# A fused attention and two-layer expert kernel: the expert layer's work list is written anew, and one unit's output is computed in another form

## The chip, the cores and the metric

The kernel runs on one core of one Trainium2 chip. Its metric is the device time of one execution in microseconds: 1166.03 us, the median of three runs (1165.91 to 1166.03).

## The reference, cut to what matters

Three layers follow each other. The first is attention over pooled memories (batch 4, 8 heads, 576 positions), and its result is `x` with 2304 tokens of 512 features. The second is a wide layer with a cosine gate. The third, the expert layer, is the one that the change is about:

```python
def _moe2_ref(x, domain_probs, w1, w2):      # x [2304, 512], w1 [4, 512, 1024], w2 [4, 1024, 512]
    p = domain_probs / (domain_probs.sum(-1, keepdims=True) + 1e-09)
    out = np.zeros((N, D), dtype=np.float32)
    for e in range(E):
        h = np.maximum(x @ w1[e], 0.0)
        out += p[:, e:e + 1] * (h @ w2[e])
    return out
```

## The kernel before, in words

Each product of two fp32 matrices is made of three TensorE passes over a high and a low part of each factor (`mm3`, line 500): high by high, high by low, low by high. A low part is a subtraction on VectorE (DVE) or GpSimd (POOL), a high part a copy on ScalarE (ACT).

The expert layer cuts the hidden features of all experts into 16 slices `s` of 256 features, the tokens into two halves `u` of 1152, and each half into two blocks `j` (512 and 640 tokens). That makes 64 units, worked through one after the other. A unit has four kinds of task, and their names are the words of a list:

- `H12` (`hidden`) makes the hidden activations of unit 12 with seven TensorE products of six matmuls each (256 or 320 columns). `R12` (`rectify`) applies the relu.
- `P12` (`pair_prep`) makes from these, on ACT, DVE and POOL, the seven operands `ht` that the output needs, each split into a high and a low part. `Q12.2` does the same for a single token tile.
- `O12.0` and `O12.1` (`pair_out`) each make the output of two token tiles of 128 tokens with seven products of three matmuls of 256 columns, in place of two full ones: sums of some operands are multiplied instead. Their order in TensorE's queue is m1, m5, m6, m2, m7, m3, m4. They accumulate in one PSUM tile `op` with the quarters pz, px and py. Three DVE instructions (`gather`, line 1274) read that tile, scale by the token's expert share and add to the sum `acc` in SBUF: e1 stands between m2 and m7 and reads px and py, e2 between m3 and m4 reads the same two, e3 after m4 reads pz and px. So m7, which adds to px again, has to wait for e1, and m4 for e2. In a profile m5, m6, m7 and m3 read `op<-wt,ht`, and m1, m2 and m4 read `op<-wb,ht`.
- `O12.2` (`plain_out`) makes the output of one token tile in full, with six matmuls of 512 columns and one `gather`. A unit that `WHOLE` names (line 306) has all of its four or five tiles worked in this way, without a `P` task: units 0, 30 and 31 of the 64.

Other words are the splitting of the input for a half (`X01`, `X10`, `X11`), of weights in the first half (`wa11`, `wb11`, `Ea8`, `Eb8`), and weights' transfers on SP's DMA queue (`get..`, `keep..`, `fetch..`). In the first half the split weights are also stored in DRAM, and the second half only loads them.

What sets the order is `LIST` (line 134), written out by hand or by a search: some 3600 words, each of which issues the next instruction or instruction group of its task. A stroke behind a word (`P3'`) takes DVE in place of POOL for a step that may go to either. So `LIST` fixes every engine's queue; each engine works its queue in order, and the waits between engines are set when the program is built, from the tiles that the instructions read and write. The tasks also name what they depend on (the last arguments of `gather`, `either`, `pe`); in the listed stage these names serve whoever makes the list, and `have(...)` only says before which point a word may not stand.

Of the kernel before, what the change touches and what calls it, by code (L numbers as in the profile page):

```python
# [138 lines left out]
P2 P2' H3 H3 H3 P2 Q2.2 Eb7 O1.1 H3 O1.1 Eb7 O1.0 Eb7' O1.0 H3 O1.0 Eb7 Ea7 Eb8 H3 R3 O1.1 Ea7 keepwb0 O1.0 O1.1 O1.1
Q2.2 O1.0 R3 R3 O1.1 Ea7 O1.0 R3 O1.1 H3 P2 O1.1 O1.0 R3 O1.1 Ea7 O1.0 H4 O1.1 Ea7 O2.0 O2.0 Ea7' O2.1 O2.0 O2.1 P3'  # L140
Ea7 Ea7 O2.0 P3 keepwt0 O2.0 P3' O2.1 O2.2 Ea7' P3 P3 O2.0 Ea7 O2.1 O2.2 H4 H4 P3 P3 P3 Ea7 P3 H4 H4 O2.1 O2.1 O2.1 P3
O2.1 Ea7 O2.0 O2.1 O2.0 H4 H4 Q3.2 O2.0 P3 Ea7 Ea7 O2.1 O2.0 H4 getwb2 O2.0 Ea7 getwa3 H4 O2.1 getwt2 O3.0 H4 R4 Ea7
# [297 lines left out]
def tile_kernel(  # L440
# [854 lines left out]
    def make_wa(s):  # L1295
# [10 lines left out]
        for f in mixes:  # L1306
            o4 = yield either(416, 740, f, o, t1, free=BW[s > TURNS[0] // 2])
# [76 lines left out]
    def early(s, kind, before):  # L1384
# [491 lines left out]
```

## Time and profile before

| what | value |
|---|---|
| median of three runs | 1166.03 us |
| the profiled execution | 1163.89 us |
| its span, first to last instruction | 1162.1 us |
| TensorE matmuls (PE) busy | 1119.0 us, 96% |
| VectorE (DVE) busy | 870.7 us, 75% |
| ScalarE (ACT) busy | 624.8 us, 54% |
| GpSimd (POOL) busy | 582.5 us, 50% |
| the expert layer, in the span | from 378.3 to the end |
| its first half of tokens | 378.3 to 764.6 |

PE stands for TensorE's matmuls and PEld for its weight loads, which run ahead of them. A matmul's busy time includes its way through the array, so matmuls that follow each other overlap and PE looks busy across short pauses; the idle time before a weight load shows a pause more fully. A row of the timeline merges instructions of one kind that follow each other; the bracket is the idle time of that engine before it and who ended it.

### The profile page before, as it was taken

The numbers are of one execution on the slowest core, as the hardware profiler recorded it, in microseconds if no ns is written. First come the engines' busy times: TensorE is split into PE (matmuls) and PEld (weight loads), VectorE is DVE, ScalarE is ACT, GpSimd is POOL, SyncE is SP. The second block draws the span as 40 slices with busy tenths as digits, with TensorE's granted clock in tenths as the row PEclk, the third lists the DMA queues.
The fourth block names the chain that finished last, engine by engine and source line by source line (L and its number), as shares of the span: only waits on it lengthen the run. The fifth ranks groups of instructions, "written<-read, shape, count | busy, mean of one in ns | idle before, by whom it ended". The sixth has DMA issues, their size and how long they took to land.

```text
span 1162.1 us, 22606 instructions
## 1 busy us (share of the span) xinstructions
PE 1119.0 (96%) x8971; PEld 1067.8 (92%) x8971; DVE 870.7 (75%) x1344; ACT 624.8 (54%) x1297; POOL 582.5 (50%) x577
## 2 busy tenths in 40 slices
PE   9999999999999999999999999999999999999996
PEld 8689999999999999998989899999999999999995
DVE  5888989897888765788777877776757766566664
ACT  4886665566555654555646655454454544444451
POOL 1465555665677357556656684335252333323350
PEclk9999999999999999999999999999999999999999
DMA  9932556267300889698785486374533643336422
GB/s 313 369 91 57 173 173 217 68 210 263 142 19 1 308 337 375 246 350 288 259 310 191 174 308 231 120 289 158 218 136 140 233 172 136 137 145 237 172 73 82
DMA packets 58553, 230.08 MB, mean 198 GB/s; under 512 B 6992, under 2 KB 17744, under 8 KB 44112
## 3 DMA queue, kind: packets, MB, share of 16 engines
q1 hardware_dynamic: 58448, 228.65, 54.5%
q8 instruction: 70, 1.15, 0.4%
q14 instruction: 35, 0.29, 0.1%
HBM read 158.63 MB, written 69.99 MB: 197 GB/s over the span
## 4 chain that ended last, share of the span: by engine, by line
PE 89%; DVE 6%; DMA 2%; issue 1%; POOL 0%; SPq 0%; ACT 0%; DVEq 0%; POOLq 0%; ACTq 0%
PE op L503 49%; PE hp L503 33%; DVE acc L1274 4%; PE z L503 4%; PE vw_ps L790 1%; DVE ht L551 1%; DMA q<-in_qt_dram 1%; DMA kv<-in_kv_dram 1%; PE warm L926 1%; DMA raw<-in_w_out_dram 1%; PE kvp L674 0%; DVE acc L551 0%; PE sc L727 0%; SPq L531 0%; DVE wt L551 0%
## 5 line engine op out<-in xcount | busy, mean ns | idle before, releaser
L1274 DVE SCALAR_TENSOR_TENSOR acc<-op,p_all,acc 128x512 f32<-128x512 f32 x390 | 283.9, 746 | 151.3 <-PE op L503 149.0
L503 PE MATMUL hp<-x,wa 128*128 128x256 f32 (+1 forms) x2268 | 354.3, 296 | 0.9 <-DVE c L1260 0.9
L503 PEld LDWEIGHTS hp<-x,wa 128*128 128x128 f32 x2268 | 316.1, 188 | 2.7 <-DVE c L1260 1.1
L503 PE MATMUL op<-wt,ht 128*128 128x256 f32 x1440 | 228.8, 285 | 24.1 <-DVE acc L1274 21.5
L503 PEld LDWEIGHTS op<-wt,ht 128*128 128x128 f32 x1440 | 195.9, 188 | 37.0 <-DVE acc L1274 33.8
L503 PE MATMUL op<-gt,wo 128*128 128x288 f32 x1536 | 218.1, 296 | 0.0
L503 PEld LDWEIGHTS op<-gt,wo 128*128 128x128 f32 x1536 | 208.1, 188 | 4.7 <-issue 2.4
L503 PE MATMUL op<-wb,ht 128*128 128x256 f32 (+1 forms) x1194 | 205.2, 294 | 5.4 <-DVE acc L1274 4.9
L503 PEld LDWEIGHTS op<-wb,ht 128*128 128x128 f32 x1194 | 171.8, 188 | 12.1 <-DVE acc L1274 6.5
L534 ACT ACTIVATE c<-c 128x256 f32<-128x256 f32 (+1 forms) x122 | 53.7, 444 | 186.8 <-DVE c L1260 186.6
L551 POOL TENSOR_TENSOR sm<-c,sm 128x256 f32<-128x256 f32 x65 | 54.5, 838 | 130.2 <-DVE sm L551 103.6
L503 PE MATMUL hp<-attnT,vw 128*128 128x288 f32 x768 | 113.2, 296 | 0.3 <-DVE attnT L551 0.3
L503 PEld LDWEIGHTS hp<-attnT,vw 128*128 128x128 f32 x768 | 105.2, 188 | 3.5 <-issue 1.6
L551 POOL TENSOR_TENSOR ht<-sm,ht 128x512 fp32r<-128x512 f32 x66 | 91.7, 1393 | 32.8 <-ACT ht L534 32.7
L551 POOL TENSOR_TENSOR gt<-y,gt 128x576 fp32r<-128x576 f32 x41 | 60.1, 1466 | 78.2 <-ACT gt L534 75.3
L897 DVE TENSOR_TENSOR acc<-op,acc 128x576 f32<-128x576 f32 (+1 forms) x120 | 84.9, 711 | 17.3 <-PE op L503 15.9
L551 POOL TENSOR_TENSOR ht<-c,ht 128x256 fp32r<-128x256 f32 (+1 forms) x68 | 70.7, 1045 | 41.5 <-ACT ht L534 41.5
L534 ACT ACTIVATE ht<-sm 128x512 fp32r<-128x512 f32 x120 | 73.9, 625 | 13.0 <-POOL sm L551 8.5
L551 POOL TENSOR_TENSOR sm<-c 128x512 f32<-128x512 f32 x21 | 27.3, 1302 | 90.8 <-ACT c L534 72.2
L534 ACT ACTIVATE u<-hp 128x320 f32<-128x320 f32 (+1 forms) x126 | 50.2, 407 | 38.7 <-PE hp L503 38.1
L1260 DVE TENSOR_TENSOR c<-hp,u 128x320 f32<-128x320 f32 (+1 forms) x126 | 56.3, 452 | 18.2 <-PE hp L503 17.0
L534 ACT ACTIVATE ht<-c 128x512 fp32r<-128x512 f32 (+2 forms) x128 | 63.0, 517 | 6.0 <-PE op L503 4.9
(152 smaller groups left out, 1558.7 us busy)
## 6 DMA issues: line engine op xcount, KB each, us to landing
wa<-wa_d SPq DMA_DIRECT2D x27, 1792.0 KB, 8.5
wb<-wb_d SPq DMA_DIRECT2D x27, 1024.0 KB, 7.3
wt<-wt_d SPq DMA_DIRECT2D x27, 1024.0 KB, 7.2
wa_d<-wa SPq DMA_DIRECT2D x10, 1792.0 KB, 11.4
raw<-in_w_dram SPq DMA_DIRECT2D x32, 512.0 KB, 6.7
wt_d<-wt SPq DMA_DIRECT2D x10, 1024.0 KB, 10.5
wb_d<-wb SPq DMA_DIRECT2D x10, 1024.0 KB, 8.4
wa_d<-acc SPq DMA_DIRECT2D x18, 512.0 KB, 4.4
```

The lines of the kernel that those rows point to most:

```text
L503: nc.tensor.matmul(out=ps, lhsT=lt(a), rhs=rt(b), start=first and i == 0, stop=last and i == 2, skip_group_check=more,)
L534: return Op("ACT", ns, fn or (lambda: nc.scalar.activation(out=out, in_=in_, func=func, **kw)), *deps, table=table)
L551: eng.tensor_tensor(out=out, in0=in0, in1=in1, op=op)
L790: nc.tensor.matmul(out=ps[32 * i:32 * i + 32, g, j * FS:j * FS + FS], lhsT=kvT[b][64 * g:64 * g + 64, 1, i, :], rhs=wi[s][0][64 * g:64 * g ...
L897: e = yield dve(155 + 301 * nd, lambda: nc.vector.tensor_tensor(out=dst, in0=op[:, :, :TH], in1=dst, op=ALU.add), o)
L926: nc.tensor.matmul(out=warm[:, :128], lhsT=ones, rhs=ones, start=True, stop=True)
L1260: return dve(157 + 1.045 * n, lambda: nc.vector.tensor_tensor(out=out, in0=ps, in1=sb, op=ALU.add), *deps)
L1274: nc.vector.scalar_tensor_tensor(out=dst, in0=ps, scalar=pe, in1=dst, op0=ALU.mult, op1=ALU.add)
```

## The change

Three things change, and nothing before the expert layer's list.

`LIST` is another list of the same tasks. One unit fewer is named in `WHOLE`: unit 30, the last slice but one, 640 tokens, first half, now has two pairs and one single tile in place of five full ones. And the tasks name more dependences: e1 of a pair names m2 beside m6, a gather into a token tile names the gather of the slice before it, and has to stand behind it, the four sums of a weight name each other, and the two tiles that unit 1 borrows name a few more of their readers.

```diff
 LIST = """
-X01 H0 X01 H0 park H0 Eb7 H1 H0 X01' H0 H0 X01' H0 H0 H0 X01 H0 X01' X01 H1 X01 H0 R0 R0 H0 R0 H1 H1 H1 keepwa0 R0
...
-WHOLE = ((0, 0, 0), (0, 14, 1), (0, 15, 1))
+WHOLE = ((0, 0, 0), (0, 15, 1))
...
+        o4 = None
         for f in mixes:
-            o4 = yield either(416, 740, f, o, t1, free=BW[s > TURNS[0] // 2])
+            o4 = yield either(416, 740, f, o, t1, o4, free=BW[s > TURNS[0] // 2])
...
-                R["raw2"].give(kr, Join([o4, lo]))
-        R["te"].give(kt, lo)
+                R["raw2"].give(kr, Join([o4, *los]))
+        R["te"].give(kt, Join(los))
...
-        c22 = yield sum_(n, c[:, 1, n:], px[:, :n], u3, o7, a5, tc_)
+        c22 = yield sum_(n, c[:, 1, n:], px[:, :n], u3, o7, a5, tc_, *([o3] if i == 1 else []))
...
-        g = yield gather(DM, outv[:, ti, :], op, p_, s == 0, o, done["x", u, 1])
+        if s:
+            yield have(("sum", ti, s - 1))
+        g = yield gather(DM, outv[:, ti, :], op, p_, s == 0, o, done["x", u, 1], done.get(("sum", ti, s - 1)))
+        todo.set(("sum", ti, s), g)
...
         m2 = yield prod(pz, 1, 1)
-        e1 = yield gather(DM, db, duo[:, 2 * HD2:], pb, first, m6)
+        if s:
+            yield have(("sum", ib, s - 1))
+        e1 = yield gather(DM, db, duo[:, 2 * HD2:], pb, first, m6, m2, done.get(("sum", ib, s - 1)))
         m7 = yield prod(px, 4, 5, e1)
...
-        e3 = yield gather(DM, da, duo[:, HD2:3 * HD2], pa, first, m4)
+        if s:
+            yield have(("sum", ia, s - 1))
+        e3 = yield gather(DM, da, duo[:, HD2:3 * HD2], pa, first, m4, done.get(("sum", ia, s - 1)))
+        todo.set(("sum", ia, s), e3)
```

What the new list does is read from the order of the built programs. The first place is TensorE's queue at unit 5's first pair. Before, its tile is `op_5853` and that of the unit's second pair `op_5888`; `hp` and `z` are products of `H6`:

```order
L503 MATMUL op_5853<-wt_5552,ht_5720 128x256 x3
L503 MATMUL op_5888<-wt_5552,ht_5720 128x256 x3
L503 MATMUL hp_5841<-x_5014,wa_5543 128x320 x6
L503 MATMUL op_5853<-wb_5539,ht_5720 128x256 x3
L503 MATMUL op_5853<-wt_5552,ht_5720 128x256 x6
L503 MATMUL op_5888<-wt_5552,ht_5720 128x256 x3
```

The first row is m6, the fourth m2, and the fifth m7 with m3: m7 stood directly behind m2.

In the new list the same pair has the tile `op_5886`, the second pair `op_5918`, and `op_5961` is the unit's single tile:

```order
L504 MATMUL op_5886<-wt_5562,ht_5733 128x256 x3
L504 MATMUL op_5918<-wb_5566,ht_5733 128x256 x3
L504 MATMUL hp_5823<-x_5013,wa_5497 128x320 x6
L504 MATMUL op_5918<-wt_5562,ht_5733 128x256 x3
L504 MATMUL hp_5815<-x_5014,wa_5497 128x320 x6
L504 MATMUL op_5918<-wt_5562,ht_5733 128x256 x3
L504 MATMUL op_5918<-wb_5566,ht_5733 128x256 x3
L504 MATMUL op_5886<-wb_5566,ht_5733 128x256 x3
L504 MATMUL op_5961<-wb_5566,h1_5774 128x512 x6
L504 MATMUL op_5886<-wt_5562,ht_5733 128x256 x6
```

Now a whole single tile of six 512-column matmuls stands between m2 (the eighth row) and m7 (the last).

The second place is TensorE's queue at unit 48, in the second half. Before, `op_11671` is the first pair and `op_11685` the second:

```order
L503 MATMUL op_11685<-wt_11415,ht_11572 128x256 x3
L503 MATMUL hp_11717<-x_9166,wa_11428 128x256 x6
L503 MATMUL op_11685<-wb_11452,ht_11572 128x256 x3
L503 MATMUL op_11671<-wb_11452,ht_11572 128x256 x3
L503 MATMUL op_11685<-wt_11415,ht_11572 128x256 x6
```

The second pair's m2 is the third row and its m7 the fifth: one product, the first pair's m4, stood between them.

In the new list the pairs are `op_11692` and `op_11771`:

```order
L504 MATMUL op_11771<-wt_11470,ht_11604 128x256 x3
L504 MATMUL op_11771<-wb_11493,ht_11604 128x256 x3
L504 MATMUL op_11692<-wt_11470,ht_11604 128x256 x3
L504 MATMUL hp_11745<-x_9284,wa_11482 128x256 x6
L504 MATMUL op_11692<-wt_11470,ht_11604 128x256 x3
L504 MATMUL op_11771<-wt_11470,ht_11604 128x256 x6
```

Two pair products and one product of `H50` now stand between the second pair's m2 (second row) and its m7 (last row).

The third place is the end of DVE's queue. Before, `op_13483` and `op_13509` are the pairs of unit 62, the other tiles single ones of unit 63, and the last TensorE product of the program is the m4 that writes `op_13509`:

```order
L1274 SCALAR_TENSOR_TENSOR acc_70<-op_13509,p_all_78,acc_70 128x2x256
L1274 SCALAR_TENSOR_TENSOR acc_70<-op_13570,p_all_78,acc_70 128x512
L1274 SCALAR_TENSOR_TENSOR acc_70<-op_13483,p_all_78,acc_70 128x512
L1274 SCALAR_TENSOR_TENSOR acc_70<-op_13581,p_all_78,acc_70 128x512
L1274 SCALAR_TENSOR_TENSOR acc_70<-op_13509,p_all_78,acc_70 128x512
```

Only the last of these five reads what the last product wrote.

In the new list the pairs of unit 62 are `op_13501` and `op_13538`, and the last TensorE product is the m4 that writes `op_13501`:

```order
L1275 SCALAR_TENSOR_TENSOR acc_70<-op_13583,p_all_78,acc_70 128x512
L1275 SCALAR_TENSOR_TENSOR acc_70<-op_13501,p_all_78,acc_70 128x512
L1275 SCALAR_TENSOR_TENSOR acc_70<-op_13616,p_all_78,acc_70 128x512
L1275 SCALAR_TENSOR_TENSOR acc_70<-op_13538,p_all_78,acc_70 128x512
L1275 SCALAR_TENSOR_TENSOR acc_70<-op_13604,p_all_78,acc_70 128x512
L1275 SCALAR_TENSOR_TENSOR acc_70<-op_13594,p_all_78,acc_70 128x512
```

Now the gather that needs the last product is the fifth from the end, and four stand behind it.

## Rows read from the trace of the kernel before

**Rows 1.** The page: the span; each engine's busy time, share, instructions.
```profile
span 1162.1 us, 22606 instructions
PE 1119.0 (96%) x8971; PEld 1067.8 (92%) x8971; DVE 870.7 (75%) x1344; ACT 624.8 (54%) x1297; POOL 582.5 (50%) x577
```

**Rows 2.** By stage: PE, PEld, DVE, ACT, POOL busy; granted clock, DMA share, GB/s.
```profile
0.00:378.30 378.30, 374.67 (x3472) 350.91 (x3473) 319.40 (x510) 237.77 (x375) 220.80 (x235) 1.00 0.48 161
378.30:764.60 386.30, 366.87 (x2705) 352.90 (x2704) 293.98 (x447) 209.36 (x488) 219.36 (x209) 1.00 0.74 268
764.60:1153.90 389.30, 377.49 (x2797) 364.00 (x2795) 255.59 (x386) 177.67 (x434) 142.30 (x135) 1.00 0.43 163
```

**Rows 3.** The page's weight-load groups: busy, mean ns | idle before, releaser.
```profile
L503 PEld LDWEIGHTS op<-wt,ht 128*128 128x128 f32 x1440 | 195.9, 188 | 37.0 <-DVE acc L1274 33.8
...
L503 PEld LDWEIGHTS op<-wb,ht 128*128 128x128 f32 x1194 | 171.8, 188 | 12.1 <-DVE acc L1274 6.5
```

**Rows 4.** Who waited for whom: us in total, times, longest.
```profile
PEld op L503 <- DVE acc L1274: 40.3, 58, 2.0
```

**Rows 5.** Timeline, unit 5's first pair: start, us, engine [idle before].
```profile
457.17 0.87 PE L503 MATMUL op<-wt,ht 128*128 128x256 f32 x6
...
458.76 0.52 PE L503 MATMUL op<-wb,ht 128*128 128x256 f32 x3
459.31 0.75 DVE L1274 SCALAR_TENSOR_TENSOR acc<-op,p_all,acc 128x512 f32<-128x512 f32 x1 [2.24 <-PE op L503]
...
460.12 1.13 PEld L503 LDWEIGHTS op<-wt,ht 128*128 128x128 f32 x9 [1.05 <-DVE acc L1274]
...
461.30 0.52 PE L503 MATMUL op<-wb,ht 128*128 128x256 f32 x3
```

**Rows 6.** Timeline, unit 48's two pairs and the products behind them.
```profile
976.53 0.77 PEld L503 LDWEIGHTS op<-wt,ht 128*128 128x128 f32 x6 [0.34 <-DVE acc L1274]
...
979.13 0.87 PE L503 MATMUL op<-wb,ht 128*128 128x256 f32 x6
...
980.49 0.78 PEld L503 LDWEIGHTS op<-wt,ht 128*128 128x128 f32 x6 [0.70 <-DVE acc L1274]
...
981.32 1.04 PE L503 MATMUL hp<-x,wa 128*128 128x320 f32 x6
...
982.20 0.87 PE L503 MATMUL op<-wb,ht 128*128 128x256 f32 x6
...
982.90 0.88 PE L503 MATMUL hp<-x,wa 128*128 128x256 f32 x6
```

**Rows 7.** Timeline: m7 of two pairs, three pair products between.
```profile
620.48 0.77 PEld L503 LDWEIGHTS op<-wt,ht 128*128 128x128 f32 x6 [0.39 <-DVE acc L1274]
...
693.91 1.12 PEld L503 LDWEIGHTS op<-wt,ht 128*128 128x128 f32 x9 [1.08 <-DVE acc L1274]
```

**Rows 8.** Timeline, unit 12's first pair: its m4, with DVE and POOL.
```profile
543.66 1.72 POOL L551 TENSOR_TENSOR ht<-sm,ht 128x512 fp32r<-128x512 f32 x1
...
544.17 1.49 DVE L551 TENSOR_TENSOR ht<-c,ht 128x256 fp32r<-128x256 f32 x1
...
546.37 0.42 PEld L503 LDWEIGHTS op<-wb,ht 128*128 128x128 f32 x3 [1.80 <-DVE acc L1274]
```

**Rows 9.** Timeline, unit 32: hidden products, first operand on POOL.
```profile
768.85 2.52 PE L503 MATMUL hp<-x,wa 128*128 128x256 f32 x18
...
773.82 1.75 POOL L551 TENSOR_TENSOR ht<-c,ht 128x512 fp32r<-128x512 f32 x1
```

**Rows 10.** Timeline, the end: the last PE and DVE rows.
```profile
1151.99 1.91 PE L503 MATMUL op<-wb,ht 128*128 128x512 f32 x9
1152.19 3.38 DVE L1274 SCALAR_TENSOR_TENSOR acc<-op,p_all,acc 128x512 f32<-128x512 f32 x5 [0.70 <-PE op L503]
```

**Rows 11.** Timeline: a DVE step on 128x256 in the turn of the halves.
```profile
772.55 0.43 DVE L551 TENSOR_TENSOR sm<-c,sm 128x256 f32<-128x256 f32 x1
```

**Rows 12.** The 50 us with most DMA in the expert layer; DMA stands last.
```profile
400.00:450.00 50.00, 47.64 (x356) 46.06 (x355) 33.67 (x56) 28.14 (x68) 29.82 (x30) 1.00 0.93 341
```

More of the change, by code (lines that the diff above doesn't have):

```diff
@@ L210 @@
-O28.1 X10 H30 O28.1 R30 X10 R30 O29.0 X10 X10 O29.0 R30 O29.1 O29.0 O29.1 R30 O29.0 O29.1 R30 O29.0 R30 X10' O29.1
-O29.1 O29.0 H31 H31 O29.1 H31 H31 R30 O29.1 X10' O29.1 H31 H31 X10 O29.1 X10 H31 O29.1 fetchwa0 O29.0 O29.0 O29.1
-O29.0 H31 H31 O29.0 O29.0 H31 R31 R31 O30.0 R31 R31 X11 R31 R31 X11' O30.1 R31 X11 O30.0 O30.2 O30.1 O30.3 X11' O30.2
-X11 O30.4 X11' X11 X11 O30.3 H32 O30.4 fetchwb0 fetchwa1 O31.0 fetchwt0 X11' fetchwt1 H32 H32 X11 H32 X11' X11 H32 H32
-X11 O31.0 H32 X11 H32 H32 X11 H32 R32 H32 R32 R32 R32 R32 P32' P32 O31.1 P32' P32 P32 P32 O31.2 O31.1 P32 P32 P32'
@@ new lines @@
+R1 O0.0 Eb7 O0.1 O0.3 P1' P1 Eb7 O0.2 Eb7 H2 P1' H2 Eb7 Eb7 O0.3 P1 P1 H2 Ea7 H2 H2 Eb7' P1 H2 P1' Eb7 H2 Eb7 H2 P1
+P1' P1' H2 P1 H2 R2 H2 R2 R2 Eb7' R2 O1.0 H3 getwa2 R2 P2' P2 Eb7 O1.0 Eb7 H3 P2 H3 Eb7' O1.1 P2 P2 O1.0 P2 H3 Eb7
+Ea7' H3 Eb8 O1.0 O1.1 Ea7 O1.0 O1.0 Ea7 O1.1 O1.0 H3 H3 O1.1 Q2.2 P2' P2 P2 O1.1 H3 Ea7 O1.1 O1.0 Q2.2 O1.0 H3 H3 R3
+Ea7 O1.1 Ea7 O1.0 O1.1 R3 R3 O1.1 P2 Ea7 O1.0 O1.1 P2 H4 Ea7 R3 O1.0 O1.1 H3 O1.1 Ea7' O2.0 R3 O2.1 Ea7 P3 P3 O2.0
+keepwb0 O2.1 O2.0 keepwt0 O2.2 O2.1 P3 O2.0 O2.1 P3 P3 Ea7 P3 P3' O2.2 H4 H4 Ea7' P3 O2.0 P3' Q3.2 Ea7 H4 H4 getwa3
@@ new lines @@
+O9.0 O9.1 Ea9' P10 P10 P10 O9.2 O9.0 Ea9 Ea9 getwa6 P10' H11 H11 Ea9 P10 P10' O9.0 O9.1 Ea9 H11 Eb10 O9.1 O9.2 H11
+O9.1 P10' O9.0 Eb10' H11 H11 O9.0 Eb10 P10' O9.1 Eb10 O9.0 O9.1 H11 O9.0 Eb10 O9.1 O9.1 Eb10 H11 O9.1 H11 R11 O10.0
+Eb10 Eb10 Eb10 O10.0 R11 R11 Ea10 O9.1 R11 H11 getwb6 O9.1 O10.0 Eb10 O10.0 R11 O10.0 P11 P11 O10.1 O10.0 H12 Eb10
+Q11.2 O10.1 P11 O10.0 Q11.2' H12 H12 O10.1 P11' P11 P11 H12 Eb10' H12 O10.1 P11' Eb10 Eb10 O10.1 Eb10 O10.0 O10.1 H12
+H12 P11 O10.0 H12 Eb10 Ea10' getwa7 O10.1 Ea10 O10.1 H12 H12 R12 P11 O10.0 H12 P11 P11' O10.1 R12 R12 O10.0 O10.1 R12
@@ new lines @@
+P19 Q19.2' H20 P19 O18.0 P19 P19 O18.1 O18.1 H20 H20 O18.1 P19 P19 O18.1 Ea15 O18.0 H20 O18.0 P19 O18.1 P19 O18.0
+O18.1 O18.0 H20 H20 R20 Ea15 O18.0 O18.1 O18.1 O18.0 O18.1 wa11 wb11 getwt10 H21 Ea15 R20 R20 wa11 O18.0 O18.1 H20
+O18.1 wa11 O19.0 O19.0 wa11' wa11 R20 R20 O19.1 P20' P20 O19.1 O19.2 P20' O19.1 wa11 O19.0 wa11 wa11' wa11 P20' O19.1
+O19.1 P20 H21 wa11 O19.1 H21 P20 O19.2 O19.0 O19.0 wa11 O19.1 O19.0 H21 H21 P20' P20 O19.0 P20' P20 O19.0 H21 H21 P20
+O19.0 O19.1 H21 O19.1 O19.0 O19.1 O19.0 H21 wb11 wa12 wb11 wb11 wb11' O20.0 H21 wb11 R21 O20.0 R21 H21 O20.0 O19.1
@@ new lines @@
+wb12 P22 wb12 wb12 O21.0 H23 wb12' wb12 wb12' wb12 H24 R23 O21.1 R23 O22.0 R23 O22.0 wb12' R23 O22.1 O22.1 P23' P23
+H24 O22.1 P23' O22.0 O22.1 Q23.2 wb12' H24 O22.1 O22.0 wa13 wb13 keepwb11 O22.0 H24 H24 wa13 H24 P23 P23 P23 P23'
+O22.0 O22.1 H24 O22.0 wa13' O22.0 P23 O22.1 P23' wa13 H24 wa13 O22.0 O22.1 P23 H24 O22.1 P23 O22.0 H24 R24 wa13 wa13
+O22.1 O22.0 H24 O22.1 O23.0 keepwt11 O23.0 Q23.2' keepwa12 O23.1 R24 R24 O23.0 O23.1 wa13' R24 O23.2 R24 P24' P24
+O23.1 wa13' P24 H25 P24 P24 P24 H25 H25 P24 P24 H25 H25 O23.0 P24 O23.1 O23.1 H25 H25 O23.1 P24 O23.2 O23.0 P24 O23.1
@@ new lines @@
+O27.0 O27.1 O27.0 O27.1 H29 O27.1 O27.0 O27.1 H29 H29 R29 O27.0 O27.1 getwt15 H29 getwb15 R29 R29 O28.0 R29 O28.1 R29
+O28.0 P29 P29 H30 O28.0 O28.1 O28.0 P29 O28.0 H30 P29 P29 H30 P29 P29' O28.1 O28.0 H30 P29 P29' H30 H30 H30 O28.0
+O28.1 O28.1 H30 O28.1 P29' O28.0 O28.1 O28.0 O28.1 H30 H30 R30 O28.1 H30 R30 R30 P29' R30 O28.0 R30 O28.1 O28.0 H31
+P30 P30 Q30.2 O29.0 Q30.2' O29.0 P30 H31 O28.1 P30' P30 O29.0 H31 P30 O29.0 P30' O29.1 P30 O29.1 P30' O29.0 H31 H31
+O29.1 O29.0 P30' P30 X10 O29.1 O29.0 X10' O29.1 O29.0 O29.1 X10 H31 H31 O29.0 O29.1 X10' O29.1 O29.0 O29.0 O29.1 X10
@@ new lines @@
+H31 O29.0 O29.1 X10 X10 H31 fetchwa0 H31 X10' O30.0 O29.1 O30.0 X10 O29.1 H31 O30.0 R31 O30.0 R31 fetchwa1 X10 O30.1
+R31 O30.1 X10' X10 O30.0 R31 O30.2 X10 O30.0 O30.1 X10 R31 R31 X10' O30.1 O30.0 R31 O30.1 O30.0 X10' O31.0 O30.1 X10
+O30.0 X10 O30.1 O30.2 O30.1 O30.0 O30.1 O31.1 X11 O30.0 X11 O31.0 O31.2 O31.1 X11' O30.1 O31.3 fetchwt0 O30.1 X11
+fetchwt1 O31.2 O31.0 O31.4 fetchwb0 O31.3 X11 O31.1 O31.2 H32 X11' X11 O31.3 H32 X11' H32 H32 H32 X11' H32 H32 O31.4
+X11 H32 O31.4 X11 X11 H32 fetchwb1 H32 R32 H32 R32 R32 X11' R32 H33 R32 P32' P32 H33 H33 P32' H33 P32' P32 P32 P32'
@@ new lines @@
+H33 H33 H33 P32 P32' H33 P32' X11 P32' H33 X11' X11' H33 R33 X11 R33 X11' O32.0 O32.0 O32.1 O32.1 H33 O32.0 R33 O32.0
+R33 R33 O32.0 H34 O32.0 P33' H34 H34 P33 P33 H34 O32.1 P33 P33 H34 H34 P33 P33 P33 O32.0 P33' O32.0 H34 O32.1 P33
+O32.1 H34 O32.1 H34 H34 R34 P33' O32.1 R34 R34 O32.1 H34 O32.0 R34 O32.1 O32.0 fetchwa2 R34 H35 O32.0 O32.1 P34 H35
+O32.1 P34 P34 H35 O33.0 Q34.2 O33.1 P34 Q34.2' O33.1 O33.0 O33.1 H35 O33.0 P34 H35 O33.0 P34 P34' O33.0 H35 P34 O33.0
+P34 H35 P34' O33.1 O33.0 P34 H35 O33.1 O33.0 H35 H35 R35 O33.1 O33.0 O33.1 R35 R35 O33.1 O33.0 R35 O33.1 H35 O33.0
@@ new lines @@
+O33.1 fetchwa3 R35 H36 O33.1 O34.0 P35' P35 O34.1 O34.1 P35' O34.0 O34.1 P35 O34.2 P35 P35 P35 P35 O34.1 O34.0 O34.2
+H36 H36 P35 O34.0 O34.0 P35 O34.1 O34.0 H36 H36 Q35.2 P35 O34.1 O34.0 O34.0 Q35.2' H36 H36 O34.0 O34.1 O34.1 O34.0
+O34.1 H36 O34.0 H36 H36 R36 O34.1 R36 R36 H36 fetchwb2 O34.1 R36 fetchwt2 O35.0 R36 O35.1 P36' P36 O35.1 O35.0 O35.1
+P36 O35.2 P36 P36 P36 H37 P36 P36 P36' P36' O35.0 H37 H37 O35.1 O35.2 H37 H37 H37 H37 O35.1 H37 O35.0 O35.0 H37 H37
+R37 P36' O35.0 H37 R37 R37 O35.1 R37 O35.0 R37 O35.0 O35.1 O35.0 O35.1 H38 O35.1 O35.0 O35.1 P37 O35.0 H38 fetchwb3
@@ new lines @@
+O40.1 P41' P41 H42 P41 O40.0 H42 O40.1 P41' H42 H42 Q41.2 O40.1 H42 H42 P41 O40.0 O40.0 H42 O40.0 H42 H42 R42 O40.0
+R42 R42 O40.1 O40.0 R42 O40.1 H43 O40.1 O41.0 O40.1 O41.0 O40.1 H42 O41.0 O41.0 R42 O41.1 P42' P42 O41.0 O41.1 P42'
+O41.2 P42' P42 P42 O41.1 O41.0 H43 O41.2 P42' P42 P42 H43 P42 H43 H43 P42 H43 H43 O41.1 O41.1 O41.0 O41.1 O41.0 H43
+O41.0 O41.1 O41.0 O41.1 O41.0 H43 H43 R43 O42.0 R43 O42.0 O41.1 H43 O42.0 R43 R43 O41.1 fetchwa7 R43 O42.0 O41.1
+fetchwt6 O42.0 P43 P43 H44 fetchwb6 O42.0 H44 H44 P43' O42.1 P43 P43 P43 P43' H44 Q43.2 H44 O42.0 Q43.2 O42.1 H44 H44
@@ new lines @@
+O42.1 P43 P43' P43 O42.1 O42.0 P43 O42.1 O42.0 H44 O42.1 H44 H44 R44 O42.0 R44 R44 O42.1 O42.0 R44 O42.1 H45 O42.1
+O43.0 O42.1 O43.0 O42.1 H44 O43.0 O43.1 R44 O43.0 P44' P44 O43.1 O43.0 P44' O43.2 P44' P44 P44 O43.0 P44' P44 P44
+O43.1 H45 H45 O43.1 P44' H45 H45 P44' O43.0 O43.0 O43.1 O43.0 H45 H45 O43.1 H45 O43.0 O43.1 O43.1 H45 H45 R45 O43.0
+O43.1 O44.0 R45 O44.0 O43.2 O43.1 O44.0 H45 R45 fetchwb7 O43.1 R45 O44.0 fetchwa8 R45 O44.1 P45' P45 fetchwt7 O44.0
+O44.1 O44.0 P45 H46 O44.1 Q45.2 O44.0 P45 P45 H46 H46 P45 P45 H46 H46 P45 P45' O44.1 P45 O44.0 H46 H46 O44.0 Q45.2
@@ L289 @@
+O62.0 O62.1 R63 O61.2 O62.1 O62.0 O62.1 O62.0 Q63.0 O62.1 Q63.1 Q63.0' O62.1 Q63.2 Q63.1' Q63.3 O63.0 O62.1 Q63.4
+Q63.3 O62.0 Q63.4 O62.1 O63.0 O63.1 Q63.2' O62.1 O63.2 O62.1 O63.1 O62.1 O63.3 O62.0 O29.1 O62.1 O63.4 O62.0 O62.0
+O63.4 O62.1 O63.3 O63.2 O63.3 O62.1 O63.1 O63.4 O63.2 O62.0 O63.0
 """.split()
@@ L1344, in make_wb @@
         h = yield a_(1024, t[:, 0], r, ACTF.Copy, o, tb)
+        o4 = None
         for f in sums2_of(tt, q[:, 0, 0], q[:, 0, 1], q[:, 1, 0], q[:, 1, 1]):
-            o4 = yield either(416, 740, f, o, t1, free=BW[s > TURNS[0] // 2])
+            o4 = yield either(416, 740, f, o, t1, o4, free=BW[s > TURNS[0] // 2])
         js = []
@@ L1403, in early @@
                       tv[:, 512 * c:512 * c + 512]) for c in range(2)]
-        os_, o4 = {}, None
+        os_, o4, los = {}, None, []
         for f in fs:
@@ L1750, in pair_out @@
             yield d
+        todo.set(("sum", ib, s), e2)
         m4 = yield prod(px, 6, 2, e2)
```

255 lines of the change are left out of this document (105 added, 150 removed).

## Prediction

> **What bounds the kernel now.** I read the page first. PE is busy for 1119.0 of 1162.1 us, and no other engine for more than 75% [rows 1]. So the time is TensorE's work plus TensorE's pauses, and an engine that works less is worth nothing by itself. The stretches say where the pauses are [rows 2]: the layers before the list lose 3.6 us in 378.3, which the change does not touch, the first expert half 19.4 us in 386.3, the second 11.8 us in 389.3, and 8.2 us follow the last matmul. The granted clock is 1.00, the level of 2.4 GHz, in each of them, so a pause costs its own length and nothing is to be had from the clock.
>
> Who ends the pauses stands in the weight loads' groups [rows 3] and in the waits [rows 4]: 40.3 us before weight loads of `op` are ended by DVE's accumulation, in 58 pieces. 33.8 us of it stand before `op<-wt,ht`, which is m7 (waiting for e1), and 6.5 before `op<-wb,ht`, mostly m4 (waiting for e2). No other wait of the list comes near it.
>
> Then one such wait is looked at in the timeline [rows 5]. m6 is the first half of the row at 457.17; another pair's product and one of `H6` follow; m2 starts at 458.76 and ends at 459.28. e1 starts at 459.31, though DVE had been idle for 2.24 us. e1 reads nothing that m2 writes (px and py against pz), but all three are one tile, and the trace shows that e1 waits for m2, not for m6. So what decides is how much TensorE work stands between m2 and m7. m7's loads start at 460.12, 1.36 us after m2. A pair product takes 0.35 us of TensorE (six matmuls from 982.20 to 982.90 [rows 6]), so 1.01 us have to be filled between the two.
>
> **The change part by part.**
>
> *m2 to m7.* From 458.76 to 461.30 stand four pair products, 1.42 us of work in 2.54 [rows 5]: with nothing between, a pair loses 1.12 us, the 1.01 and 0.11 for the slower start of the matmuls behind a wait. With work between, it loses 1.12 less that work. At unit 48 one pair product (0.35) stood between: 0.77, and the rows from 979.13 to 981.32 have 1.41 us of work in 2.19, which is 0.78 [rows 6]. A 256-column product of a hidden task or two pair products fill 0.70: 0.42, where the idle time is 0.34 [rows 6]. A 320-column product fills 0.88 (981.32 to 982.20 [rows 6]): 0.24. Counted in TensorE's order before, 14 of 120 pairs have nothing between, 13 one pair product, 18 the 0.70 us (three of them lose nothing, as the other pair's wait stands just ahead), and 4 the 0.88 us. The sum over these 49 is 14 x 1.12 + 13 x 0.77 + 15 x 0.42 + 4 x 0.24 = 33.0 us. By idle time alone (1.05, 0.70, 0.34, and 0.2 as an estimate for the last) it is 29.7 of the 33.8 us [rows 3, 5, 6].
>
> In the new order none of 122 pairs has less than 1.06 us between: three pair products (18 pairs), or more. So all 49 waits go: **-33.0**. What is late next is DVE itself. The other 71 pairs of before lose 33.8 - 29.7 = 4.1 us in all, 0.058 each, where e1 stands behind a long DVE step. 51 more pairs in that class make 51 x 0.058 = **+3.0**. Bounds: 0, and 8 from the tightest kind: before, eight pairs had just three pair products between, and two of them lost 0.39 and 1.08 [rows 7], 0.18 over the eight; by that rate ten more cost 1.8, on top of a doubled rate for the others. I take 3.0, the rate of the whole class.
>
> *m3 to m4.* The work between them is as long as before, 1.7 us on average. Its 6.5 us [rows 3] are mainly three waits such as the 1.80 us one [rows 8], where e2 stood behind a DVE step of 1.49 us beside a POOL step of 1.72. All three came in pairs whose m7 had also waited, so their DVE queue was already out of its place. I take half, **-3.0**; bounds -6.5 and +6.5 (as many again, with PE pressing DVE more).
>
> *Unit 30.* Five full tiles go, each six matmuls of 512 columns, 1.40 us as twice the 0.70 of 256 columns [rows 6]; 14 pair products of 0.35 and one tile come: 6.3 for 7.0, **-0.7**. The new `P30` and `Q30.2` put eleven and two steps on ACT, DVE and POOL. They are hidden by 10.7 us of products that now stand between `H30` and `O30.0`; without these the chain would show.
>
> *Unit 32*, the first of the second half, has less cover: 4.3 us of products between its last hidden one and its m1, 10.6 before. In the trace its last hidden product is the last third of the row at 768.85 and over by 771.0, and the first operand is ready at 775.57, 4.6 us later [rows 9], with 1.75 us on POOL for a step that DVE takes now. I take 0, bounds 0 and 2.
>
> *The end.* Before, DVE ended at 1155.57, 1.67 us after PE's last row at 1153.90 [rows 10], because only one gather needed the last product. Now five need it or stand behind one that does. The five in the row took 3.38 us, so DVE ends 3.4 us behind PE: **+1.7**; bounds 0 and 2.5.
>
> *The rest.* The named dependences issue no instruction. DVE has 17 steps more in the list and POOL ten fewer; their cover is DVE's idle time, 92 us in the first half [rows 2], and without it the first rival's case is there. The transfers are the same 183 in another order. The tightest load is unit 4's `wa`: between `H2`'s last product, which frees its buffer, and `H4`'s first stand 10.2 us of products now, 11.4 before. No product waited for a load before, so I take 0, bounds 0 and those 1.2.
>
> The sum: -33.0 + 3.0 - 3.0 - 0.7 + 1.7 = -32.0. The profiled execution took 1163.9 us, 1.8 us of it outside the span, so 1131.9; the median of the runs was 2.1 above it, which I add: **1134 us**.
>
> One thing speaks for a smaller gain. A DVE step on 128x256 takes 0.43 us in one place [rows 11] and 1.49 beside a running POOL step in another [rows 8]. The Trainium skill, "SBUF — State Buffer", section "Who interferes with whom", states that a DVE instruction with two SBUF inputs contends with a GpSimd instruction that reads SBUF, and that one of the two waits out the other's whole instruction. The trace agrees, by the 1.49 us. By that rule each of the 17 steps given to DVE can wait out a POOL step, and the time would be the first rival's.
>
> **The rivals.**
>
> *DVE binds the first half.* It is busy 294.0 of 386.3 us there [rows 2]. If the 17 steps all land there at 1.49 us [rows 8], 25 us are added, and the half is to lose some 17 of its 19.4 us of pauses: 319 of 369, 86%. Then e1 and e2 stand behind a long step more often; ten more waits like the 1.80 us one [rows 8] give back 18 us: 1152. For it: the three long waits. Against it: DVE's idle 2.24 us ahead of a late e1 [rows 5], time lost to the order and not to load.
>
> *Slower: weights late in the first half.* DMA is busy 0.93 of 400 to 450 [rows 12] and 0.74 over the half [rows 2]. If the loads can't be had sooner, the first products of the 11 slices that are loaded there wait: at 3.3 us each, 36 us, all the gain and more, 1170. It decides from a DMA share near 1. A half shorter by 4% asks for 0.97 in the busiest 50 us, so it hardly comes to that.
>
> *The new distance does nothing,* if e1 is late for a reason other than m2. Then -0.7 and +1.7 remain: 1167. Against it: e1 starts 0.03 us after m2's end, with DVE idle [rows 5].
>
> **How the numbers follow.** The forecast, with 1123 to 1142 as its own range (the lower end with m4's bound and with the remaining waits and the end at nothing), has 0.82; DVE binding, 1142 to 1154, has 0.13; late weights 0.03, of which 0.01 ends still faster; no effect 0.02, half of it within 0.2%. The range of 1123 to 1147 leaves out about 0.16. About 0.2%, 2.3 us, is what a measurement of this kernel can tell from no change: faster 0.96, within it 0.01, slower 0.03.
>
> **What would show it.** Right: DVE's accumulation ends under 12 us of weight-load idle time in place of 40.3, `op<-wt,ht` has under 8 us of it, both halves take 368 to 378 us, and the last DVE row ends some 3.4 us after PE's. Wrong: many waits of 1 us before `op<-wt,ht` are left (then m2 was not it), waits of 1.5 to 2 us before `op<-wb,ht` with long DVE steps ahead (DVE binds), or `hp` products that wait for a DMA.

## The result: 38.7 us faster, and the profile after

The changed kernel takes 1127.27 us (median of six runs, 1124.34 to 1131.57); the kernel before took 1165.97 beside it. The ratio is 0.9667, 95% interval 0.9642 to 0.9692. In a second series it was 1126.09 us, ratio 0.9656 (0.9637 to 0.9676). 1134 was forecast, with 1123 to 1147 as the range: the time lies inside it, and the gain is some 7 us larger than forecast.

The first profile of the changed kernel is that of its slowest run, 1131.57 us. The page's first lines, to be held against [rows 1]:

```profile
span 1129.8 us, 22652 instructions
PE 1110.7 (98%) x8989; PEld 1069.8 (95%) x8989; DVE 875.4 (77%) x1361; ACT 628.5 (56%) x1305; POOL 580.9 (51%) x567
```

By stage, as in [rows 2] (layers before the list, first and second expert half; columns as there):

```profile
0.00:385.26 385.26, 380.02 (x3472) 355.49 (x3473) 319.99 (x510) 237.80 (x375) 219.52 (x234) 0.99 0.46 158
385.26:755.80 370.54, 366.83 (x2753) 357.10 (x2752) 300.47 (x463) 211.85 (x496) 223.72 (x205) 1.00 0.78 289
755.80:1119.90 364.10, 363.88 (x2767) 357.26 (x2765) 251.60 (x384) 178.86 (x436) 137.70 (x128) 1.00 0.43 165
```

The first half got 15.8 us shorter and the second 25.2; in the second, PE is now busy for all but 0.2 us. The first row went the other way: the list starts at 385.3 us, not at 378.3. Two stretches of the early layers, span and columns as above, show why (this profile):

```profile
20.00:30.00 10.00, 10.00 (x105) 8.93 (x97) 6.43 (x16) 3.75 (x8) 2.54 (x4) 0.83 0.93 312
35.00:50.00 15.00, 13.49 (x140) 9.11 (x144) 13.26 (x34) 12.38 (x21) 10.04 (x11) 0.81 1.03 366
```

The mean granted clock was 0.83 and 0.81 there: the level of 1.2 GHz for 3.4 us from 20.3 on and for 6.8 us from 44.2 on (the second reaches 1.0 us past its stretch). Before the first of them TensorE had paused more than in the kernel before (busy 16.6 of the first 20 us, there 18.7). As an estimate, 10.2 us at half the clock cost up to 5.1 us, and with the 2.0 us of pauses that is about what the list starts late. The profile of the second series, a run of 1124.28 us, has none of it, and there the list starts at 378.8:

```profile
0.00:378.77 378.77, 374.69 (x3473) 350.98 (x3474) 318.82 (x510) 237.69 (x375) 219.13 (x234) 1.00 0.47 161
378.77:748.37 369.60, 366.90 (x2754) 357.12 (x2752) 300.27 (x463) 211.78 (x496) 223.59 (x205) 1.00 0.78 290
748.37:1112.60 364.23, 364.03 (x2767) 357.41 (x2765) 251.64 (x384) 178.72 (x436) 137.59 (x128) 1.00 0.42 165
```

So the 7 us belong to that execution and not to the change. Where the list itself gained is in the weight loads' groups, the two of [rows 3], and in the waits, [rows 4], again of the first profile (the change moved every line by one):

```profile
L504 PEld LDWEIGHTS op<-wt,ht 128*128 128x128 f32 x1464 | 200.0, 188 | 5.9 <-DVE acc L1275 2.2
...
L504 PEld LDWEIGHTS op<-wb,ht 128*128 128x128 f32 x1182 | 169.1, 188 | 5.5 <-DVE acc L1275 1.5
```

```profile
PEld op L504 <- DVE acc L1275: 3.7, 9, 1.2
...
PEld op L504 <- DMA wt<-wt_d: 1.7, 1, 1.7
```

40.3 us in 58 waits became 3.7 in nine. Unit 5, the pair of [rows 5], now reads so in the timeline:

```profile
462.83 0.87 PE L504 MATMUL op<-wb,ht 128*128 128x256 f32 x6
...
463.55 1.57 PE L504 MATMUL op<-wb,h 128*128 128x512 f32 x6
463.75 1.41 DVE L1275 SCALAR_TENSOR_TENSOR acc<-op,p_all,acc 128x512 f32<-128x512 f32 x2 [0.97 <-PE op L504]
...
464.72 1.61 PEld L504 LDWEIGHTS op<-wt,ht 128*128 128x128 f32 x12
```

The row at 462.83 is m2 of both pairs, a full tile of 1.4 us follows, and DVE's row is e1 of both. m7's weights load at 464.72 without a pause, where before the same row had 1.05 us of idle time.

### The profile page after: what moved, and what is told of

Its sections match the earlier page's. It is cut to its first block, busy times and chain, and to the rows that moved or that the text cites. A ratio compares the mean times of both kernels' runs of the same rounds, so it can differ in the third digit from the quotient of the medians.

```text
span 1129.8 us, 22652 instructions
## 1 busy us (share of the span) xinstructions
PE 1110.7 (98%) x8989; PEld 1069.8 (95%) x8989; DVE 875.4 (77%) x1361; ACT 628.5 (56%) x1305; POOL 580.9 (51%) x567
## 4 chain that ended last, share of the span: by engine, by line
PE 92%; DVE 3%; DMA 2%; issue 1%; ACT 1%; POOL 1%; SPq 0%; DVEq 0%; POOLq 0%
PE op L504 49%; PE hp L504 34%; PE z L504 4%; DMA q<-in_qt_dram 2%; PE vw_ps L791 1%; DMA wt<-wt_d 1%; PE warm L927 1%; DVE acc L1275 1%; PE kvp L675 1%; PE spare L919 1%; PE sc L728 0%; DVE x L552 0%; DVE sm L552 0%; DVE ht L552 0%; SPq L532 0%
## 5 line engine op out<-in xcount | busy, mean ns | idle before, releaser
L504 PEld LDWEIGHTS op<-wt,ht 128*128 128x128 f32 x1464 | 200.0, 188 | 5.9 <-DVE acc L1275 2.2
L504 PE MATMUL op<-wb,ht 128*128 128x256 f32 (+1 forms) x1182 | 201.8, 291 | 0.3 <-DVE acc L1275 0.2
L504 PEld LDWEIGHTS op<-wb,ht 128*128 128x128 f32 x1182 | 169.1, 188 | 5.5 <-DVE acc L1275 1.5
L552 POOL TENSOR_TENSOR sm<-c 128x512 f32<-128x512 f32 x34 | 44.3, 1302 | 127.5 <-ACT c L535 109.4
L552 POOL TENSOR_TENSOR ht<-sm,ht 128x512 fp32r<-128x512 f32 x64 | 88.9, 1391 | 28.9 <-ACT ht L535 28.7
L552 POOL TENSOR_TENSOR ht<-c,ht 128x256 fp32r<-128x256 f32 (+1 forms) x62 | 67.7, 1097 | 21.5 <-ACT ht L535 18.1
L535 ACT ACTIVATE op<-op 128x256 f32<-128x256 f32 x122 | 44.7, 368 | 48.5 <-PE op L504 45.2
L535 ACT ACTIVATE ht<-c 128x256 fp32r<-128x256 f32 (+1 forms) x129 | 64.1, 516 | 11.5 <-PE op L504 10.3
```

Of the source, the lines that this page charges most:

```text
L504: nc.tensor.matmul(out=ps, lhsT=lt(a), rhs=rt(b), start=first and i == 0, stop=last and i == 2, skip_group_check=more,)
L535: return Op("ACT", ns, fn or (lambda: nc.scalar.activation(out=out, in_=in_, func=func, **kw)), *deps, table=table)
L552: eng.tensor_tensor(out=out, in0=in0, in1=in1, op=op)
```

## The experiments

Lines put into a kernel shift its line numbers, so `gather` is not at L1274 in each.

### The distance alone

```diff
...
+for name in PAIRS:
+    m6 = 4 if name in ("O1.0", "O1.1") else 3
+    LIST.insert(at(name)[m6], LIST.pop(at(name)[m6 + 1]))
```

`PAIRS` names the 49 pairs with under 1.01 us between m2 and m7; `at(name)` gives the places of a task's words in `LIST`.

> The kernel before with its own list; in the 49 pairs with under 1.01 us of products between m2 and m7, m2 alone is moved forward, to directly behind m6. Nothing of the new list is taken. If e1 waits for m2 and only the products between m2 and m7 cover it, the sum of 1.12 us less that work falls from 34.2 to 6.7 us over all pairs (13 pairs keep 0.70 us between), so -27.5, and up to -5.4 more if the three long m4 waits, which all stand in these pairs, were a consequence of the late e1: 1133 to 1139 us. If the rest of the new list (unit 30, other places of the steps of DVE and POOL) made the gain, the time stays within 3 us of 1166.

Measured: 1140.29 us, ratio 0.9781 (0.9757 to 0.9804), 25.2 us less and 1.3 above the range expected. Its two groups:

```profile
L517 PEld LDWEIGHTS op<-wt,ht 128*128 128x128 f32 x1440 | 196.7, 188 | 15.7 <-DVE acc L1288 13.5
L517 PEld LDWEIGHTS op<-wb,ht 128*128 128x128 f32 x1194 | 171.9, 188 | 8.4 <-DVE acc L1288 2.7
```

Moving 49 words gave two thirds of the gain, so at most a third is left for all else in the new list. From the list's first matmul to the start of its last, 775.3 us became 748.8: -26.5 for the -27.5 of the distances. Pair by pair in TensorE's order, the 16 pairs that still have less than 1.01 us wait for 5.3 us and start 1.6 slower; 6.7 were left to them by the prices. Of the three long m4 waits, those of units 12 and 20 went and that of unit 15 (1.72 us) stayed, so only some followed from a late e1. What the forecast had not looked at is that 13 other pairs wait for 6.8 us in all with 1.05 us of work and more between m2 and m7.

### m2 behind m7

```diff
-        m2 = yield prod(pz, 1, 1)
...
         m7 = yield prod(px, 4, 5, e1)
+        m2 = yield prod(pz, 1, 1)
```

In `LIST`, m2's word of each pair goes directly behind m7's. (z1 is ACT's copy between m5 and m6.)

> The kernel before with its own list, but m2 is issued behind e1 and m7 in every pair (m1, m5, z1, m6, e1, m7, m2, m3), its place in TensorE's order directly behind m7's. Then e1 can wait for m6 at most, and what counts is the work between m6 and m7 without m2: 12 pairs have 0.70 us there, one 0.88, all others over 1.01. If e1 waited for m2 only because m2 is issued ahead of it into the same tile, 5.3 us of waits stay of 34.2: -28.9 and up to -5.4 for the m4 waits, 1132 to 1137 us. If e1 was late for another reason (DVE's load, its own place in DVE's order), the time stays within 5 us of 1166.

Measured: 1136.30 us, ratio 0.9745 (0.9719 to 0.9771), 29.2 us less, as expected. Unit 5's first pair:

```profile
459.23 0.87 PE L514 MATMUL op<-wt,ht 128*128 128x256 f32 x6
...
459.85 0.75 DVE L1285 SCALAR_TENSOR_TENSOR acc<-op,p_all,acc 128x512 f32<-128x512 f32 x1 [0.36 <-PE op L514]
...
460.82 0.52 PE L514 MATMUL op<-wt,ht 128*128 128x256 f32 x3
...
461.18 0.52 PE L514 MATMUL op<-wb,ht 128*128 128x256 f32 x3
```

e1 runs at 459.85, after m6 (first half of the row at 459.23) and 1.33 us before m2 starts at 461.18; m7, at 460.82, does not wait. So e1 does not need m2; it waited where m2 was issued ahead of it into the same tile. The built programs say the same: before, e1 waits for the count of matmuls at m2's last one in 111 of the 120 pairs, and here at m6's last one in 105 (in the others an earlier step of DVE has already waited as far). In 99 of these 105 other products are issued between m6 and e1, and e1 does not wait for them: it is the tile that counts, not the order of issue alone.

The parts came out a little otherwise than the sum. In the profiles m7 lost 26.2 us less (28.9 was expected) and m4 6.0 less, some 3 us came on at m6 and at hidden products, and the list as a whole went from 775.3 to 746.0 us.

### The distance taken away again

```diff
...
+for name in PAIRS:
+    m2, e1, m7 = at(name)[4:7]
+    LIST.insert(m7 - 1, LIST.pop(e1))
+    LIST.insert(m7 - 1, LIST.pop(m2))
```

`PAIRS` names 30 pairs here, one in four.

> The changed kernel; in 30 of its 122 pairs m2 and e1 are moved back to directly before m7, so that no product stands between m2 and m7. If the distance is what the new list gained by, each of the 30 loses 1.12 us, 1.05 of it idle time of the weight loads of m7: +33.6, 1158 to 1163 us. If the new list gained by something else, the 30 pairs cost little: 1127 to 1132 us.

Measured: 1158.70 us, ratio 0.9941 (0.9918 to 0.9964): 31.4 us more than the changed kernel's 1127.27. The list's 734.3 us became 767.6, +33.3 for the +33.6 forecast. The waits, and the pair of unit 5 among the 30:

```profile
PEld op L518 <- DVE acc L1289: 34.2, 37, 1.9
```

```profile
459.96 0.51 PE L518 MATMUL op<-wb,ht 128*128 128x256 f32 x3
460.51 1.41 DVE L1289 SCALAR_TENSOR_TENSOR acc<-op,p_all,acc 128x512 f32<-128x512 f32 x2 [1.71 <-PE op L518]
461.31 0.77 PEld L518 LDWEIGHTS op<-wt,ht 128*128 128x128 f32 x6 [1.04 <-DVE acc L1289]
```

In 28 of the 30 pairs m7 starts 1.00 to 1.01 us later than it would right behind the 0.35 us of work of the product ahead of it (its weight loads stand idle for 1.04 to 1.05); in the other two it is 1.40 and 1.86. So the price of a pair is right from both sides, put in and taken out.

### 34 more steps on DVE

```diff
...
+for step in STEPS:
+    name, ns = step.split(":")
+    at = [k for k, w in enumerate(LIST) if w.rstrip("'") == name]
+    for n in map(int, ns.split("+")):
...
+        LIST[at[n]] += "'"
```

`STEPS` names 34 steps of `P` words, units 1 to 29, that POOL did before.

> The changed kernel; 34 steps of the first half that split an operand (subtractions and sums of two SBUF tiles) go from POOL to DVE, about 25 us more for DVE if each takes 0.75 us, and 90% of the half in place of 81%. This is the first rival's case, with the load that it assumed. By it e1 and e2 stand behind long DVE steps more often and some ten waits like the one of 1.8 us come: +18 us, about 1145. If DVE's load does not decide as long as DVE has idle time and e1 has its 1.06 us, it costs 0 to 4 us: 1127 to 1131.

Measured: 1134.78 us, ratio 0.9733 (0.9706 to 0.9760), 7.5 us more than the changed kernel: between the two. Its first half and its waits:

```profile
378.91:757.89 378.98, 370.12 (x2753) 357.61 (x2752) 319.81 (x497) 211.06 (x496) 190.09 (x171) 1.00 0.76 283
```

```profile
PEld op L514 <- DVE acc L1285: 10.1, 19, 1.4
```

DVE got 19.3 us of work and not the 25 that were expected, and is busy for 84% of the half and not 90%; the half took 8.4 us more, 0.25 us a step. The weight loads' waits for gathers are ten more and 6.4 us longer, six of the ten before m4. So DVE is not the bound at 84%, but its added steps already cost time, most of it through the gathers that queue behind them. My bound for "no cost" (4 us) was too low; the rival's 18 was too high for the 319.8 us that DVE has here, which is the load of the prediction's rival (319), and the 90% are not tried.

### The order in DVE's queue

The kernel of the distance alone, with six more words moved:

```diff
...
+for name, n, behind, m in (("O61.0", 5, "O61.0", 4), ("O15.0", 8, "O15.0", 7), ("Q25.2", 1, "O24.1", 5),
+                           ("O26.1", 5, "O26.0", 5), ("O28.1", 5, "O28.1", 4), ("O11.1", 5, "O11.1", 4)):
...
```

The word n of a task goes directly behind the word m of another.

> The kernel before with the 49 m2 moved forward as in the run on the distance alone, and in six places the order of DVE's steps mended as well: at units 61 and 15 a gather that could run stood behind a gather that was still waiting for its own m2, at units 11, 24, 26 and 28 the gather e1 stood behind another step of DVE that it could have passed. Nothing else moves. These six waits are 1.66, 1.72, 0.59, 1.04, 0.76 and 0.49 us in the profile of the run on the distance alone, 6.3 us in all. If what the distance leaves is the order in DVE's queue, 5 to 6.3 us go: 1134 to 1135 us where that run had 1140.3. If it is DVE's load, the waits turn up at the next products and the time stays within 1.5 us of 1140.

Before this edit, unit 61 in the profile of the distance alone shows such a wait:

```profile
1107.07 0.52 PE L517 MATMUL op<-wb,ht 128*128 128x256 f32 x3
...
1108.32 0.51 PE L517 MATMUL op<-wb,ht 128*128 128x256 f32 x3
...
1108.87 1.41 DVE L1288 SCALAR_TENSOR_TENSOR acc<-op,p_all,acc 128x512 f32<-128x512 f32 x2 [2.28 <-PE op L517]
...
1110.33 0.77 PEld L517 LDWEIGHTS op<-wt,ht 128*128 128x128 f32 x6 [1.70 <-DVE acc L1288]
```

The m2 at 1107.07 is that of O61.0, whose e1 could run at 1107.6. But DVE's next step in order is e1 of O61.1, whose m2 only comes at 1108.32; so DVE stands idle for 2.28 us, does both, and m7 of O61.0 is 1.70 us late.

Measured: 1134.61 us, ratio 0.9734 (0.9708 to 0.9760), 5.7 us less than the distance alone. In the two profiles the list went from 748.8 to 744.9, 3.9 us: of the six waits, 6.3 us in all, only 0.2 at unit 11 is left, and new ones of 0.63 (m1 of unit 16) and 0.75 us (m4 of unit 28) came next door. So most of it was the order, and a third of it came back. What is left to the changed kernel, 7.3 or 8.5 us by the two medians, is mostly the 6.9 us that the 16 pairs with a short distance still lose.

### The changed kernel again, and with four repairs

> The changed kernel once more, as it is. Its first profile lost 7 us in the layers ahead of the list, where the granted clock was at half for 3.4 and 6.8 us and transfers were late. If that was chance (the instructions there are those of before), the list starts at 378 to 380 us in most executions and the time is 1124 to 1128; if the changed kernel always pays for it, the list starts at 385 us again and the time is 1130 to 1132.

Measured: 1126.09 us (1124.28 to 1128.04), its list's start at 378.8 us (shown above). The early instructions are the same in all kernels here, and of the seven other profiles six have the list's start between 378.0 and 379.6; the seventh, with m2 behind m7, has it at 383.1 and half the clock for 6.8 us as well. The kernel before has such executions too: its runs of 1168.3 to 1171.0 us beside these experiments have a mean clock of 0.994 to 0.996, the others, up to 1167.6 us, 0.997 to 0.999. So it comes with single executions and not with the change; what sets it off is not shown.

The repairs move `getwt6`, a step of `wa12` (with the load `wb12` behind it) and one of `X10`, and rewrite the end:

```diff
-Q63.3 O62.0 Q63.4 O62.1 O63.0 O63.1 Q63.2' O62.1 O63.2 O62.1 O63.1 O62.1 O63.3 O62.0 O29.1 O62.1 O63.4 O62.0 O62.0
-O63.4 O62.1 O63.3 O63.2 O63.3 O62.1 O63.1 O63.4 O63.2 O62.0 O63.0
+Q63.3 O62.0 Q63.4 O62.1 O63.0 O63.1 Q63.2' O62.1 O63.2 O62.1 O63.1 O62.1 O63.3 O62.0 O29.1 O63.2 O62.1 O62.0
+O63.3 O62.1 O63.4 O62.0 O63.4 O63.0 O63.1 O63.2 O63.3 O62.1 O62.0 O63.4
...
+for name, n, behind, m in (('getwt6', 0, 'getwa7', 0), ('wa12', 1, 'O20.0', 8), ('wb12', 0, 'wa12', 1), ('X10', 1, 'O29.0', 8),):
...
```

> The changed kernel with four repairs of what its profile still shows. (1) The last words: the sum of O62.0 no longer stands ahead of four others in DVE's order, and its last product comes before the last full tile, so that DVE ends 0.8 us behind TensorE's last row and not 3.4: -2.6. (2) The load of wt for slice 6 is issued behind that of wa for slice 7, some 7 us earlier: the wait of 1.7 us of unit 12's m5 goes, unless the transfers beside it are slowed as much. (3) and (4) At units 20 and 29 a long DVE step is put behind the two gathers that it delayed: -0.8 and -0.7. In all -5.8, 1121 to 1122 us; if what is in the way at these places is DMA's share and DVE's load and not the order, the waits turn up next door and only the end's 2.6 is left: 1124 to 1125.

Measured: 1118.69 us, ratio 0.9597 (0.9575 to 0.9619), 7.4 us less than the changed kernel beside it, 47 less than before and 2.3 below the range expected. The end of the changed kernel, which answers to [rows 10]:

```profile
1114.77 5.07 PE L504 MATMUL op<-wb,ht 128*128 128x512 f32 x24
...
1115.75 10.65 SPq L532 DMA_DIRECT2D out_dram<-acc  x10
1119.87 3.38 DVE L1275 SCALAR_TENSOR_TENSOR acc<-op,p_all,acc 128x512 f32<-128x512 f32 x5 [3.49 <-PE op L504]
...
1122.62 3.77 SPq L532 DMA_DIRECT2D out_dram<-acc  x7
```

The row at 1122.62 is the later part of the row at 1115.75. The end of the repaired one:

```profile
1105.19 5.08 PE L513 MATMUL op<-wb,ht 128*128 128x512 f32 x24
...
1106.17 5.85 SPq L541 DMA_DIRECT2D out_dram<-acc  x10
1108.20 2.86 DVE L1284 SCALAR_TENSOR_TENSOR acc<-op,p_all,acc 128x512 f32<-128x512 f32 x4 [0.66 <-PE op L513]
```

DVE ends 0.8 us behind PE and not 3.4, and the span ends 4.3 us after DVE (1115.4) and not 6.5. The rest of the gain is on SP's queue, which issues the stores of the result one behind another. In the changed kernel the last seven start only at 1122.62, because the first of them waits for the fourth of DVE's five last gathers (done at 1122.60); they take 3.77 us and are issued 3.1 us after DVE's end. In the repaired one the ten follow each other from 1106.17 on, and the last is issued 1.0 us after DVE's end. From there to the end of the span it is 3.4 us in both, and in the kernel before. From the last matmul's start to the end of the span it is 5.5 us, 10.2 before, and so the end gave 4.7 where 2.6 was expected. Inside the list, 733.5 us became 731.9, 1.6 us and not 3.2: the wait for `wt` was only 0.7 us in this run of the changed kernel, and at units 20, 21 and 30 waits of 0.56, 0.2 and 0.32 came for those that went.

## Why the prediction was right, and which term was off

The sum of the forecast stood against the trace, from the list's first matmul on (775.3 us before, 734.3 after, by the first profile):

| term | forecast | measured |
|---|---|---|
| m2 to m7, the 49 pairs and the waits that remain | -33.0 + 3.0 | -35.1 |
| m3 to m4 | -3.0 | -5.6 |
| unit 30 | -0.7 | -0.6 |
| unit 32 | 0 | 0 |
| all hidden products | not named | -1.1 |
| m5 of unit 12 waits for `wt` | 0 | +1.7 |
| the end | +1.7 | +1.7 |
| the layers ahead of the list | 0 | +6.9, in the second profile +0.5 |

Waits are counted here from the end of one product to the start of the next, with the slower start of the matmuls behind a wait. The rows of the list add up to 40.7 of its 41.0 us. That the first profile's span is 32.3 us shorter, just what was forecast (32.0), is luck: the list gained some 7 us more and the layers ahead of it lost as much.

**What held.** The diagnosis. In the trace of before the 49 pairs lose 28.6 us and start 4.8 slower, 33.4 for the 33.0 of the prices. That e1 waits for m2 and not for m6 is shown by m2 behind m7, the price by the distance taken out and put in again. The signs came: 3.7 us of weight-load waits for gathers (under 12 was said), 2.2 of them before `op<-wt,ht` (under 8), the first half at 370.5 us, and DVE's end 3.4 us behind PE's last row. Only the second half, at 364.1, lies below the 368 that were said.

**What failed** is the step "51 more pairs in that class make 51 x 0.058 = **+3.0**", with the 4.1 us that the other 71 pairs were to go on losing. By it 7.1 us were to remain. 3.0 remained, and 4.1 of the 7 us are here; another 1.0 is that m7 lost 38.1 us before and not 37.1. The rate as such was not too high: with the distance alone, the 104 pairs that have enough of it lost 6.8 us and 1.6 in starts, 0.08 each. I took it for a property of the class. It is a property of the list: a gather stands behind another gather that waits, or behind a long step, and six moved words took 3.9 us of such waits off the list. The new list has other places for DVE's steps as well, so that only two such waits remain. The one at unit 20, in the first profile after:

```profile
632.27 2.44 POOL L552 TENSOR_TENSOR ht<-c,ht 128x512 fp32r<-128x512 f32 x2
632.29 1.82 DVE L552 TENSOR_TENSOR wt<-tt,wt 128x512 fp32r<-128x512 f32 x1
...
634.15 0.84 DVE L552 TENSOR_TENSOR tt<-raw 128x256 f32<-128x256 f32 x1
...
634.91 1.40 DVE L1275 SCALAR_TENSOR_TENSOR acc<-op,p_all,acc 128x512 f32<-128x512 f32 x2
635.70 0.78 PEld L504 LDWEIGHTS op<-wt,ht 128*128 128x128 f32 x6 [1.17 <-DVE acc L1275]
```

Two steps of 2.7 us together, both beside POOL, and then e1: this is the first rival's wait, in two places and not in ten.

**m3 to m4**: "I take half, -3.0" was too little by 2.6. The distance alone took 3.9 (7.6 to 3.7, starts included), the order of the gathers at unit 15 another 1.7. **The hidden products** were not priced: H1 waited 1.04 us for a copy of ACT before and H24 1.02 for a DVE sum, and still do with the distance alone; 0.27 and nothing after, but an o5, another hidden product, has a new wait of 0.50. Which part of the new list did that was not tried alone. **The late `wt`** is the second rival in one place: 1.6 us, 0.7 in the second profile, and not at eleven slices. **Unit 32** is read from a row that ends at 771.37 and not at 771.0, which its 0 does not hang on.

The Trainium skill, "SBUF — State Buffer", section "Who interferes with whom", lets one of the two wait out the other's whole instruction where a DVE instruction with two SBUF inputs meets a GpSimd instruction that reads SBUF. The trace agrees: the first DVE step above takes 1.82 us beside POOL, where two others of its kind, with no POOL instruction beside them, take 0.68; the next, of half the size and beside POOL too, takes 0.84. Steps of DVE with one input in PSUM (`c<-hp,u`, 256 columns) take 0.42 us with or without POOL beside them. What the kernel paid for a step given to DVE was less than such a wait, though: 0.25 us each over the 34.

## What to carry to other kernels

A wait set when the program is built can be wider than the data: here a reader's wait took in a product issued ahead of it into the same tile, into a part that it does not read. The order in which the program issues to a tile is then part of the dependence, and moving the unneeded product behind the reader took 29.2 us off here, moving it ahead in 49 places 25.2, of the 38.7 of the whole new list. Price a list's remaining waits from what stands ahead in the waiting engine's queue, place by place, and not by a rate per pair.

## What had not been expected of the hardware

The end of the span depends on how the last stores leave, not only on when DVE is done: 6.5 us from DVE's end to the span's end where the last seven stores stand in a row whose first waits for a gather, 4.3 where they are spread over the last products; from the last store's issue it is 3.4 us in both. And the early layers can fall to the 1.2 GHz level for 6.8 or 10.2 us in one execution and not in the next, with the list 4.8 and 7.0 us later here; a difference of two single executions of that size says nothing about a change.
